# The seam between a recurrent-attention stage and a mixture-of-experts stage: one expert's rows loaded ahead of the last scatter, that scatter's rows added on TensorE

## The chip, the cores and the metric

The kernel runs on one core of a Trainium2 chip. The metric is the device time of one execution in microseconds (us), the median of several runs. All times inside the execution are counted from the start of the profiled span.

## What is computed

Three layers follow each other. The first is a recurrence over 768 steps for 4 batches of 8 heads, whose output becomes 3072 token rows of 320 numbers. The second sends each token to the expert with the largest logit, in order of arrival up to a capacity (768), and weights the expert's result with the softmax probability. The third is a dense two-layer network with an ELU.

```python
y[:, :, t] = einsum('bhd,bhde->bhe', rt, state)
Sa = einsum('bhde,bhe->bhd', state, at)
state = state * wt[:, :, None, :] - einsum('bhd,bhe->bhde', Sa, bt) + einsum('bhd,bhe->bhde', vt, kt)
...
expert_idx = argmax(x @ w_gate, axis=1)          # x: 3072 x 320, 8 experts
disp[e, counts[e]] = x[i]                        # rows of expert e in order of arrival
h = maximum(einsum('ecd,edf->ecf', disp, w1), 0) # 8 x (320 -> 1024 -> 320)
y = einsum('ecf,efd->ecd', h, w2)
out[i] = gate_w[i] * y[expert_idx[i], pos[i]]
...
h = x @ w_in                                     # 320 -> 2048 -> 320, all tokens
return where(h > 0, h, exp(minimum(h, 0)) - 1) @ w_out
```

## The kernel before

**First stage (`attention`).** The recurrence is cut into 24 units of work (two groups of heads, chunks of 64 steps), and each unit into steps with one-letter names: `q` and `y` are the products that give the output, `x` turns it into 128 token rows with their gate logits (a tile `XO` of 329 columns: 320 numbers, the token's number, 8 logits), `b` and `j` find each row's place (`SLOT`), `D` scatters `XO` with an indirect transfer on GpSimd's queue into `disp`, the array in HBM that holds each expert's rows. The order of all steps is written down by hand: a table `ORDER` for the early units and a function `slot(k)` that writes the later ones. Every engine and queue executes its own instructions in just that order. Between them stand steps named `V`: pieces of a conversion of 64-bit weights into 32-bit ones on VectorE, seven blocks here, two or three VectorE instructions a piece, with loads and stores on SyncE's queue. Twenty-one of these pieces stand in units 17 to 23; the last one stands behind the last scatter `D23`. Steps of `ahead` prepare the first half of the first expert's weights (`fetch` loads a half, `split` cuts it into a high and a low part, a cast on ScalarE and four subtractions on GpSimd for each of four pieces).

**The seam.** When the first stage ends, its buffers are given back, and the second stage's buffers lie on the same memory: the first use of such a buffer on an engine waits until all that used the old ones is done.

**Second stage (`ffn`).** Blocks of rows follow each other: 8 experts of 448 rows (4 x 112), then 6 blocks of 512 tokens for the dense network. `start` loads the first block's rows `X` from `disp`, holds TensorE busy with 26 products whose result nobody reads, turns the rows with 12 transposes into three PSUM tiles `pt`, and `prep` casts them to `XH`/`XS` on ScalarE and takes the remainder `XL` on VectorE. `run` then makes, for each of the 8 quarters f of a block, the first products (`s1`, 8 matmuls into `ph`), the second products of the quarter three before (`s2`, 8 matmuls into `po`), the ReLU of the quarter before (ScalarE writes H, VectorE writes L), a step of the next block's load, softmax (`soft`, the gate of each row) and transposes, and a piece of `split` of later weights. For block b the next block's load stands at f = 0, its softmax at f = 2, the four multiplications of its rows by the gate (L1094, ScalarE) at f = 3, its transposes at f = 4, 5 and 6. The first block alone isn't multiplied before but after its products, by a tile made in `late_gate`.

Of the kernel before, what the change touches and what calls it, by code (L numbers as in the profile page):

```python
# [33 lines left out]
ORDER = """
se1 sa0 se0 se0 v1 sc0 e0.0 sv se1 e0.1 sd p0 sw p0 e1.0 sw a0 p0 v0 p1 sa1 sx a0 p1 lw sz st1 e2.0 c0.0 a1
p2 p2 a1 c0.0 e1.1 sr1 Z7 c0.1 p1 e3.0 c0.1 k0.0 k0.1 c0.1 c1.0 e2.1 a2 a2 c1.0 p3 c1.1 k1.1 k1.0 c1.1 k1.0 e4.0 d1 k1.1
c1.1 e3.1 m0.0 l0 m0.1 k0.1 p2 p3 a3 l1 a3 p4 p4 p3 m1.1 c2.1 e5.0 k2.1 c2.0 c2.1 m1.0 r0 c2.0 k2.0 k0.0 a4 m2.1 a4 p5
st0 k2.0 k3.1 sc1 c3.0 c2.1 c3.1 ss1 k3.0 e4.1 m2.0 p4 r0 r1 c4.0 i0 e6.0 k3.0 n0 k3.1 m3.0 k4.1 p5 n1 o0 c3.1 p6
c3.0 e5.1 a5 a5 c3.1 m3.1 k2.1 r1 e7.0 l2 p5 k4.1 c4.1 k4.0 m4.1 e6.1 c4.0 c5.1 k5.1 l3 p6 k5.0 c5.0 c4.1 p7 c4.1 p6 a6
m5.0 a6 v2 v3 p7 c5.0 t1 m4.0 t0 c6.1 m6.1 c5.1 k4.0 f1 k6.1 c5.1 k6.0 k6.1 m5.1 sr0 a7 i1 c6.0 f1 f0 a7 o1 e7.1 e8.0 f1 f0  # L40
k5.0 p7 c6.1 f0 f1 f1 p8 c6.0 d0 e9.0 f0 k5.1 c7.1 f0 f1 f1 c6.1 c7.0 f0 f0 e8.1 c7.1 g1 c7.0 g0 p8 m7.0 a8 ss0 p8 m7.1
g0 k7.1 l5 l4 g1 k7.0 k7.1 g0 k8.0 g0 c7.1 l6 p9 e9.1 g1 a8 u0 m6.0 p9 k6.0 k8.1 u0 g1 l7 c8.0 k7.0 m8.0 c8.1 n2 t2 e10
w0 a9 p9 f2 n3 k8.1 a9 q0.0 w0 q0.1 q0.1 w0 i2 u1 u1 f2 q0.0 c8.0 f2 p10 k9.1 c9.1 f2 c8.1 c9.0 m8.1 k8.0 Z2 c8.1 f2 w0
Z4 p10 t3 f2 s0 k9.1 p10 c9.1 c9.0 w1 w1 k9.0 y0 f2 i2 k9.0 g2 s0 w1 e11 s0 c9.1 f3 k10.1 Z3 r2 a10 w1 a10 f3 k10.1 m9.0
f3 y0 m9.1 k10.0 p11 Z0 r2 c10.0 q1.0 q1.0 c10.1 x0 f3 p11 h2 q1.1 s1 f3 g2 a11 k10.0 m10.1 i2 f3 c10.0 g2 q1.1 c10.1 h2
e12 v4 p11 f3 s1 c10.1 x0 y1 y1 d2 g3 p12 a11 s1 k11.1 c11.0 x1 g3 r3 Z6 c11.0 g2 g3 p12 k11.1 h3 x1 m11.0 a12 Z5 p12 x0 r3
u2 a12 c11.1 c12.0 u2 g3 w2 d3 c11.1 w2 k11.0 w2 x1 k12.1 h3 q2.0 q2.1 Z1 b0 w2 c11.1 c12.1 u3 c12.1 m10.0 m11.1 s2 j0
o2 u3 w3 k11.0 q2.1 q3.1 c12.0 e13 z2 q2.0 s2 w3 y2 s2 l11 j0 l10 y2 t4 m12.0 m12.1 r4 v5 l9 g4 d4 w3 k12.1 r4 p13 D0
h4 x2 l8 g4 c12.1 k12.0 D1 h4 t5 q3.0 p13 w3 g4 g4 g4 s3 u4 x2 a13 l12 s3 z3 q3.0 u4 w4 w4 a13 q3.1 p13 i3 w4 g5 h5 y3
d5 x2 w4 y3 s3 s4 i3 k12.0 e14 t6 s4 s4 h5 v6  # L50
"""
FIRST = [f for f, n in GROUPS if f > 6]
AHEAD = (17, 19, 20, 21, 22, 23)

CV0, CVN = 17, 7


def slot(k):
    L = []
    a = lambda x: L.extend(x.split())  # L60
    live = k < NU

    nx, up = k + 1, k + (8 if k < 7 else 9)
    ups = up < NU
    pair = k - 3 if k % 2 else None
    work = {f - 6 + i: (g, i) for g, (f, n) in enumerate(GROUPS) for i in range(4) if f > 8}
    work[5] = (3, 3)
    w = work.get(k)
    if live: a(f"r{k} r{k}")
    if ups and k != 7: a(f"c{up}.0")  # L70
    if FU <= k < NU: a(f"g{k} g{k}")
    more = ups and up + 1 < NU
    if ups and k != 7: a(f"m{up}.0 c{up}.0")
    if more and k != 7: a(f"p{up+1}")
    a(f"x{k-2} x{k-2} x{k-2}")
    if k == NU: a(f"b{NU-2}.1")
    if FU <= k < NU: a(f"g{k} g{k}")
    if w and w[1]:
        a(f"i{w[0]}")
        if w[1] == 3: a(f"o{w[0]}")  # L80
    if k % 2 == 0: a(f"D{k-3}")
    second = f"c{up}.1 m{up}.1 c{up}.1 c{up}.1 p{up+1} l{up}"
    if ups: a(second if k != 7 else f"a{up} a{up} c{up}.0 m{up}.0 c{up}.0 p{up+1}")
    if k + 2 < NU: a(f"v{k+2}")
    V = (lambda: a("V")) if CV0 <= k < NU else (lambda: None)

    if nx in FIRST: a(f"t{nx}")
    a(f"q{k-1}.0 q{k-1}.0")
    V()
    if w and not w[1] and k != 6: a(f"i{w[0]}")  # L90
    if live: a(f"u{k} u{k}")
    if k == 7: a(second)
    if more: a(f"p{up+1}")
    a(f"q{k-1}.1 q{k-1}.1")
    V()
    if pair is not None: a(f"b{pair}")
    if ups:
        a(f"k{up}.0 k{up}.0 k{up}.1 k{up}.1")
    if FU <= nx < NU and nx not in FIRST: a(f"g{nx}")
    if live and k < 22: a(f"w{k} w{k} w{k} w{k}")  # L100
    if up + 2 < NU: a(f"E{up+2}")
    if more: a(f"a{up+1} a{up+1}")
    a(f"z{k-1}")
    if nx < NU: a(f"h{nx} h{nx}")
    if nx < NU: a(f"d{nx}")
    if k + 2 < NU and k + 2 not in FIRST: a(f"t{k+2}")
    if live and k < 22: a(f"s{k} s{k} s{k}")
    if k == NU: a(f"j{NU-2}.1 j{NU-2}.1 D{NU-2}")
    a(f"y{k-1} y{k-1}")
    if nx in FIRST: a(f"g{nx}")  # L110
    V()
    if pair is not None: a(f"j{pair} j{pair} D{pair}")
    if k == 6:
        up += 1
        a(f"c{up}.0 m{up}.0 c{up}.0 c{up}.1 m{up}.1 c{up}.1 c{up}.1 p{up+1} l{up} i{w[0]}")
        a(f"k{up}.0 k{up}.0 k{up}.1 k{up}.1 E{up+2} p{up+1} p{up+1}")
    return " ".join(L)

# [1373 lines left out]
```

## Time and profile before

| | |
|---|---|
| median of 3 runs | 1049.12 us (1045.7 to 1049.5) |
| the profiled execution's own time | 1045.15 us |
| its span in the trace | 1043.3 us |
| busy in the span: TensorE matmuls | 959.6 us, 92% |
| VectorE | 726.0 us, 70% |
| GpSimd | 616.3 us, 59% |
| ScalarE | 515.7 us, 49% |
| mean granted TensorE clock | 0.942 of full |

PE is TensorE's matmuls, PEld its weight loads, DVE is VectorE, ACT ScalarE, POOL GpSimd, SPq SyncE's queue. Busy time is a sum over the span; the seam lies between 425 and 465 us, and what happens there is read from the timeline, not from the sums.

### The profile page before, as it was taken

The numbers are of one execution on the slowest core, as the hardware profiler recorded it, in microseconds if no ns is written. First come the engines' busy times: TensorE is split into PE (matmuls) and PEld (weight loads), VectorE is DVE, ScalarE is ACT, GpSimd is POOL, SyncE is SP. The second block draws the span as 40 slices with busy tenths as digits, with TensorE's granted clock in tenths as the row PEclk, the third lists the DMA queues.
The fourth block names the chain that finished last, engine by engine and source line by source line (L and its number), as shares of the span: only waits on it lengthen the run. The fifth ranks groups of instructions, "written<-read, shape, count | busy, mean of one in ns | idle before, by whom it ended". The sixth has DMA issues, their size and how long they took to land.

```text
span 1043.3 us, 25335 instructions
## 1 busy us (share of the span) xinstructions
PE 959.6 (92%) x9995; PEld 868.6 (83%) x9995; DVE 726.0 (70%) x1287; ACT 515.7 (49%) x1011; POOL 616.3 (59%) x926
## 2 busy tenths in 40 slices
PE   4868978899899999989999999999999999999993
PEld 4858878798788889778888888888999889998893
DVE  8956757788674568547677777586767777677761
ACT  3646535566464334254445556465545555455551
POOL 4767929899898813377768777944333323333332
PEclk8867878899899889999999999999999999999997
DMA  6768776666665674386786766601001010100000
GB/s 163 170 171 201 167 135 124 146 138 137 131 122 117 138 192 116 118 227 192 224 225 169 225 192 206 226 24 26 26 1 52 1 26 26 26 26 1 26 2 28
DMA packets 180935, 121.67 MB, mean 117 GB/s; under 512 B 105744, under 2 KB 166824, under 8 KB 179176
## 3 DMA queue, kind: packets, MB, share of 16 engines
...
HBM read 86.87 MB, written 33.05 MB: 115 GB/s over the span
## 4 chain that ended last, share of the span: by engine, by line
PE 40%; DVE 7%; DMA 3%; ACT 3%; issue 2%; POOL 1%; SPq 0%; POOLq 0%; ACTq 0%; DVEq 0%
PE ph L970 21%; PE po L998 5%; PE po L997 5%; PE po L996 5%; DMA w<-E 2%; DVE L L1101 2%; DVE E L859 1%; ACT X L1094 1%; ACT ring L775 1%; DVE M L865 1%; DMA ring<-in_w_dram 1%; DVE N L864 1%; POOL L L1115 1%; ACT H L1100 1%; PE po L1037 1%
## 5 line engine op out<-in xcount | busy, mean ns | idle before, releaser
L780 POOL TENSOR_TENSOR ring<-ring,ring 128x64 fp32r<-128x64 f32 (+2 forms) x320 | 203.9, 674 | 75.3 <-ACT ring L775 75.3
L1115 POOL TENSOR_TENSOR L<-E,H 128x512 fp32r<-128x512 f32 x66 | 90.7, 1374 | 169.7 <-ACT H L1114 155.9
L970 PE MATMUL ph<-XH,ring 128*128 128x512 f32 (+1 forms) x640 | 170.5, 388 | 0.6 <-ACT XH L954 0.3
L1108 ACT ACTIVATE E<-N 128x512 f32<-128x512 f32 x96 | 60.8, 633 | 151.1 <-DVE N L1107 78.2
L353 POOL TENSOR_TENSOR X<-X,ring 128x60 f32<-128x60 f32 (+19 forms) x170 | 125.5, 738 | 13.3
L970 PEld LDWEIGHTS ph<-XH,ring 128*128 128x128 f32 x640 | 115.7, 189 | 14.7 <-ACT XH L954 0.6
L998 PE MATMUL po<-ring,L 128*128 128x320 f32 x384 | 119.4, 311 | 1.5 <-POOL L L1115 1.5
L996 PE MATMUL po<-ring,H 128*128 128x320 f32 x384 | 118.5, 309 | 0.2 <-ACT H L1114 0.2
L997 PE MATMUL po<-ring,H 128*128 128x320 f32 x384 | 118.5, 309 | 0.0
L970 PE MATMUL ph<-XL,ring 128*128 128x512 f32 (+1 forms) x320 | 96.7, 383 | 0.0
L970 PE MATMUL ph<-XS,ring 128*128 128x512 f32 (+1 forms) x320 | 96.5, 382 | 0.0
L351 POOL TENSOR_TENSOR ring<-X,ring 128x60 f32<-128x60 f32 (+19 forms) x108 | 69.8, 646 | 39.4 <-DMA ring<-dab 18.3
L1112 DVE SCALAR_TENSOR_TENSOR M<-E,M 128x512 f32<-128x512 f32 x96 | 79.4, 827 | 14.8 <-ACT M L1109 14.7
L1107 DVE TENSOR_SCALAR N<-ph 128x512 f32<-128x512 f32 x96 | 65.7, 684 | 27.9 <-PE ph L970 27.6
L996 PEld LDWEIGHTS po<-ring,H 128*128 128x128 f32 x384 | 72.1, 188 | 4.5 <-ACT H L1114 0.5
L997 PEld LDWEIGHTS po<-ring,H 128*128 128x128 f32 x384 | 71.9, 187 | 4.3
L998 PEld LDWEIGHTS po<-ring,L 128*128 128x128 f32 x384 | 72.1, 188 | 2.0 <-POOL L L1115 2.0
L1113 DVE SCALAR_TENSOR_TENSOR E<-ph,M 128x512 f32<-128x512 f32 x96 | 66.4, 691 | 8.1 <-DVE M L1112 0.5
L970 PEld LDWEIGHTS ph<-XL,ring 128*128 128x128 f32 x320 | 60.8, 190 | 10.9
L1101 DVE SCALAR_TENSOR_TENSOR L<-ph,H 128x448 fp32r<-128x448 f32 x64 | 39.4, 617 | 43.5 <-ACT H L1100 43.4
L970 PEld LDWEIGHTS ph<-XS,ring 128*128 128x128 f32 x320 | 60.2, 188 | 10.5
L775 ACT CAST ring<-ring 128x704 fp32r<-128x704 f32 x80 | 61.4, 778 | 12.4 <-DMA w<-GE 5.7
...
## 6 DMA issues: line engine op xcount, KB each, us to landing
...
```

Source lines behind the costliest of these rows:

```text
L351: nc.gpsimd.tensor_tensor(tv, X[:, 0:n, s:s + 1].to_broadcast([128, n, m]), N[:, s:s + 1, s + 1:e].to_broadcast([128, n, m]), op=ALU.mult)
L353: nc.gpsimd.tensor_tensor(X[:, 0:n, s + 1:e], X[:, 0:n, s + 1:e], tv, op=ALU.subtract)
L775: s.nc.scalar.copy(B[:, 0:704], r)
L780: s.nc.gpsimd.tensor_tensor(B[:, to], r[:, q], B[:, q].bitcast(F32), op=ALU.subtract)
L970: nc.tensor.matmul(p, l, r[:, 0:s.T], start=i == 0, stop=i == len(seq) - 1)
L996: nc.tensor.matmul(o, H[:, c], hb, start=f == 0, stop=False)
L997: nc.tensor.matmul(o, H[:, c], lb, start=False, stop=False)
L998: nc.tensor.matmul(o, L[:, c], hb, start=False, stop=f == s.W.nf - 1)
L1107: nc.vector.tensor_scalar(N, p, 0.0, None, op0=ALU.min)
L1112: nc.vector.scalar_tensor_tensor(out=M, in0=E, scalar=1.0, in1=M, op0=ALU.add, op1=ALU.mult)
L1113: nc.vector.scalar_tensor_tensor(out=E, in0=p, scalar=0.0, in1=M, op0=ALU.max, op1=ALU.add)
L1115: eng.tensor_tensor(L, E, H.bitcast(F32), op=ALU.subtract)
```

## The change

Five edits, all around the seam.

1. The table now holds the whole order, and is otherwise the old one, except: the pieces `V` of the last two units are closer together, so that the piece that stood behind `D23` and the one behind `y22` now stand between `q22` and `b20`; and the first half of `j22` stands before `y`'s first products of unit 23.
2. `D23` is taken out of the first stage. Unit 23's row tile is no longer one of the four `XO` buffers but a part of `DR`, which moves to the constants, so that it outlives the first stage.
3. `last_rows`: the first expert's rows are loaded (in four transfers of 112 rows instead of one of 448) without unit 23's rows, whose places hold zeros. A matrix of zeros and ones says which of unit 23's tokens belongs in which of the 448 places.
4. In `start`, 10 unread products instead of 26; then, into each of the three `pt` tiles, two products of the 0/1 matrix with the high and low part of unit 23's rows, and on top of them the loaded rows by 12 products with the identity instead of 12 transposes. `last_scatter` (the old `D23`) stands on GpSimd's queue behind the four pieces of `split(1)`.
5. `late_gate` loads the first expert's logits by themselves, after the last scatter, and its softmax and products are later (f = 5 of the first block to f = 1 of the second); of `split(2)` no piece stands at f = 0 and two stand at f = 2 and 3.

```diff
-        XO = wk.tile([128, RW], F32, tag="XO", name="XO", bufs=4)
+        XO = DR[:, 0:RW] if u == NU - 1 else wk.tile([128, RW], F32, tag="XO", name="XO", bufs=4)
...
     do(f"x{NU-1}", f"b{NU-1}.1")
     warm(6)
-    do( f"j{NU-1}.1", f"D{NU-1}", "V")
+    do(f"j{NU-1}.1")
...
+            if add:
+                oh, parts = add
+                w = [slice(128 * k, 128 * k + (128, 128, s.W2)[k]) for k in range(3)]
+                for k, c in enumerate(w):
+                    for j, x in enumerate(parts):
+                        nc.tensor.matmul(P[k][0:c.stop - c.start, 0:s.T], x[:, c], oh[:, 0:s.T], start=j == 0, stop=False)
+                for i in range(4):
+                    for k, c in enumerate(w):
+                        nc.tensor.matmul(P[k][0:c.stop - c.start, s.P * i:s.P * i + s.P], s.X[0:s.P, i, c], ident[0:s.P, 0:s.P], start=False, stop=i == 3)
...
-            nc.sync.dma_start(out=s.X[0:112], in_=src)
+            for i in range(4) if now else (slice(0, 4),):
+                nc.sync.dma_start(out=s.X[0:112, i], in_=src[:, i])
...
+        add = None if dyn else last_rows(bl[0])
         go(split(1), 5)
-        bl[0].start(0 if dyn else 26)
+        if not dyn:
+            last_scatter()
+        bl[0].start(0 if dyn else 10, add)
...
-            go(gen[0], 1 if i < 14 else 2)
+            go(gen[0], (0, 1, 2, 2)[f] if i == 0 and not dyn else 1 if i < 14 else 2)
...
+    def last_rows(B):
+        xo = cst["dr"][:, 0:RW]
+        it = ap.tile([128, 512], F32, tag="N", name="N")[:, 0:SL]
+        oh, xh, xl = (ap.tile([128, 512], F32R, tag="H", name="H", bufs=6) for _ in range(3))
+        w = slice(0, D + 1)
+        nc.gpsimd.iota(it, pattern=[[1, SL]], base=SL, channel_multiplier=0, allow_small_or_imprecise_dtypes=True)
+        nc.scalar.copy(xh[:, w], xo[:, w])
+        nc.gpsimd.tensor_tensor(xl[:, w], xo[:, w], xh[:, w].bitcast(F32), op=ALU.subtract)
+        for _ in B.load(True):
+            pass
+        f = ap.tile([128, 1], F32, name="sf", bufs=1)
+        nc.vector.tensor_copy(f, cst["slot"][:, 23:24])
+        nc.vector.tensor_scalar(oh[:, 0:SL], it, f, None, op0=ALU.is_equal)
+        return oh, (xh, xl)
...
     def late_gate(B):
-        g = yield from soft(B, "late")
+        yield
+        lg = ap.tile([128, 4, 8], F32, name="lgx", bufs=1)[0:112]
+        with nc.allow_non_contiguous_dma("the logits of a row"):
+            nc.sync.dma_start(out=lg, in_=dv[0, 1][:, :, D + 1:RW])
+        yield
+        yield
+        yield
+        g = yield from soft(B, "late", lg)
```

How it moves instructions, at the three places that matter below. First VectorE in unit 23's turn, from the mask of `q22`'s second half (`Qs`) to unit 22's output `XT`; before:

```order
L530 TENSOR_TENSOR Qs_6185<-q_6208,mask_63 128x512
L858 TENSOR_SCALAR GE1_94<-AM5_132 128x320
L859 SCALAR_TENSOR_TENSOR GE3_96<-AM5_132,GE1_94 128x320
L580 TENSOR_REDUCE mx_6217<-LG_68 128x2
...
L556 TENSOR_TENSOR XT_139<-y_6227,GE10_103 104x512
L864 TENSOR_SCALAR GE1_94<-GE3_96 128x320
L865 SCALAR_TENSOR_TENSOR GE2_95<-AM5_132,GE1_94 128x320
```

And with the change (L812 to L824 are the conversion's lines there, L486 is `Qs`, L536 begins `b20`, L512 is `XT`):

```order
L812 TENSOR_SCALAR GE1_95<-AM5_132 128x320
L813 SCALAR_TENSOR_TENSOR GE3_97<-AM5_132,GE1_95 128x320
L486 TENSOR_TENSOR Qs_6185<-q_6211,mask_63 128x512
L818 TENSOR_SCALAR GE1_95<-GE3_97 128x320
L819 SCALAR_TENSOR_TENSOR GE2_96<-AM5_132,GE1_95 128x320
L821 TENSOR_TENSOR GE2_96<-GE2_96,GE3_97 128x320
L823 TENSOR_SCALAR GE1_95<-AM5_132 128x320
L824 SCALAR_TENSOR_TENSOR GE3_97<-GE1_95,GE2_96 128x320
L536 TENSOR_REDUCE mx_6223<-LG_68 128x2
...
L512 TENSOR_TENSOR XT_139<-y_6233,GE10_104 104x512
```

Five conversion instructions that stood behind `XT` (two) and behind the last scatter (three) now stand ahead of `b20` and `XT`. Second GpSimd's queue at the seam with the change (`one`, `begin`, `turn` are small constants of the second stage, `ring4` is the half of the weights that `split(1)` cuts, L1243 the last scatter):

```order
L1418 MEMSET one_6400 128x8
L1421 IOTA begin_6402 128x1 x4
...
L1425 MEMSET turn_6409 128x1
L1232 IOTA N_6411 128x448
L1234 TENSOR_TENSOR H_6414<-DR_73,H_6413 128x321
L734 TENSOR_TENSOR ring4_6426<-ring3_6270,ring4_6426 128x64
...
L1243 DMA disp_74<-DR_73,SLOT_70 28672x329
L734 TENSOR_TENSOR ring6_6529<-ring0_6491,ring6_6529 128x64
```

Before, the scatter (L610) stood directly ahead of `one`; now it stands behind two new instructions and the 16 of `split(1)`. Third SyncE's queue with the waits of each transfer, the second block's load `X` before and, in the second fence, with the change (`DMASW` are the semaphores of GpSimd's scatters):

```order
L1087 DMA X_6512<-disp_73 112x4x329 [waits DMAHW3_49,DMAHW5_49,DVE_49,PE_49]
L801 DMA ring3_6514<-in_w1_dram 128x4x128 [waits Activation_49,Pool_49]
```

```order
L1053 DMA X_6508<-disp_74 112x4x329 [waits DMAHW6_49,DMAHW0_49,DMAHW7_49,DMASW5_49,PE_49]
L755 DMA ring3_6510<-in_w1_dram 128x4x128 [waits Activation_49,Pool_49]
```

The scatter's semaphore is now waited for by the second block's load instead of the first block's, and `fetch(3)` (`ring3`) stands behind that wait.

## Rows read from the trace of the kernel before

**Rows 1.** Busy time by stretch of 100 us (stretch, length, engines with counts, clock, DMA)
```profile
500.00:600.00 100.00, 97.12 (x490) 86.27 (x489) 74.42 (x136) 49.41 (x91) 73.85 (x115) 1.00 0.74 214
```
**Rows 2.** Timeline of TensorE, 434 to 464 us (start, length, instruction, idle before)
```profile
434.50 1.12 PE L562 MATMUL x<-IW,XT 128*128 128x88 f32 x8 [0.79 <-DVE XT L556]
...
447.31 1.71 PE L935 MATMUL pt<-ident,X 112*128 112x112 f32 x12 [3.13 <-DMA X<-disp]
...
449.31 1.92 PE L970 MATMUL ph<-XH,ring 128*128 128x448 f32 x4 [0.29 <-ACT XH L954]
...
452.08 0.98 PE L970 MATMUL ph<-XH,ring 128*128 128x448 f32 x4
...
462.89 0.55 PE L935 MATMUL pt<-ident,X 112*128 112x112 f32 x4
463.71 1.08 PE L970 MATMUL ph<-XH,ring 128*128 128x448 f32 x4 [0.27 <-DVE L L1101]
```
**Rows 3.** Stretches of 2 us: TensorE busy, granted clock, DMA share, GB/s
```profile
448.00:450.00 2.00, 1.71 (x9) 0.53 1.16 227
450.00:452.00 2.00, 2.00 (x8) 0.62 0.65 204
```
**Rows 4.** Timeline of VectorE, 425 to 440 us
```profile
425.30 0.69 DVE L530 TENSOR_TENSOR Qs<-q,mask 128x512 f32<-128x512 f32 x1 [0.31 <-PE q L525]
...
426.67 0.16 DVE L580 TENSOR_REDUCE mx<-LG 128x2 f32<-128x16 f32 x1
...
427.78 0.68 DVE L556 TENSOR_TENSOR XT<-y,GE 104x512 f32<-104x512 f32 x1
428.38 0.32 DVE L864 TENSOR_SCALAR GE<-GE 128x320 int32<-128x320 int32 x1
428.73 0.49 DVE L865 SCALAR_TENSOR_TENSOR GE<-AM,GE 128x320 f32<-128x320 uint32 x1
429.14 0.17 DVE L601 TENSOR_TENSOR rt<-rt,ebase 128x16 f32<-128x16 f32 x1
...
438.31 0.48 DVE L867 TENSOR_TENSOR GE<-GE,GE 128x320 f32<-128x320 f32 x1
...
439.06 0.49 DVE L870 SCALAR_TENSOR_TENSOR GE<-GE,GE 128x320 f32<-128x320 int32 x1
```
**Rows 5.** Timeline of GpSimd, SyncE's queue and ScalarE, 439 to 452 us
```profile
439.02 0.96 POOL L610 DMA_INDIRECT disp<-XO,SLOT  x1 [3.92 <-issue]
...
441.75 2.82 ACT L775 CAST ring<-ring 128x704 fp32r<-128x704 f32 x4 [5.66 <-DMA w<-GE]
442.47 0.34 SPq L1087 DMA_DIRECT2D X<-disp  x1
442.78 0.10 POOL L1418 MEMSET one<- 128x8 f32 x1 [2.69 <-issue]
...
443.30 8.35 POOL L780 TENSOR_TENSOR ring<-ring,ring 128x64 fp32r<-128x64 f32 x16
...
451.77 0.34 SPq L1087 DMA_DIRECT2D X<-disp  x1
```
**Rows 6.** Timeline of VectorE and ScalarE, second block's softmax and gate
```profile
456.36 0.17 DVE L1074 TENSOR_REDUCE g<-X 112x4 f32<-112x32 f32 x1
...
457.32 0.77 ACT L775 CAST ring<-ring 128x704 fp32r<-128x704 f32 x1
...
459.96 1.93 ACT L1094 ACTIVATE X<-X,g 112x320 f32<-112x320 f32 x4 [1.43 <-DVE rn L1350]
```
**Rows 7.** Groups by shape, 441 to 460 us (count, busy us, mean ns, idle before)
```profile
L780 POOL TENSOR_TENSOR ring<-ring,ring 128x213 fp32r<-128x213 f32 x14 | 8.7, 644 | 0.0
...
L1263 PE MATMUL pgate<-ident,g 112*128 112x112 f32 x8 | 1.0, 273 | 0.0
```
**Rows 8.** Groups by shape, GpSimd, whole span
```profile
L1115 POOL TENSOR_TENSOR L<-E,H 128x512 fp32r<-128x512 f32 x66 | 90.7, 1374 | 169.7 <-ACT H L1114 155.9 <-PE po L997 9.5 <-PE ph L970 4.3
```
**Rows 9.** The 24 scatters of the first stage, from issue to landing
```profile
DMA to landing us min/median/max: 2.7/4.8/7.6
```

More of the change, by code (lines that the diff above doesn't have):

```diff
@@ L39 @@
[L39 to L43, printed above, removed]
@@ L49 @@
-h4 x2 l8 g4 c12.1 k12.0 D1 h4 t5 q3.0 p13 w3 g4 g4 g4 s3 u4 x2 a13 l12 s3 z3 q3.0 u4 w4 w4 a13 q3.1 p13 i3 w4 g5 h5 y3
-d5 x2 w4 y3 s3 s4 i3 k12.0 e14 t6 s4 s4 h5 v6
-"""
[L52 to L117, printed above, removed]
@@ L145, in attention @@
     zr = sh[0][:, 2578:2798]
-    DR = one.tile([128, 520], F32, name="DR")
+    DR = cst["dr"]
     NPC = LOOK + 4
@@ L637, in attention @@
                  n=m_load, t=tt_load, f=t32, g=t64, r=rhs, u=u_solve, w=vu_tr, s=s_update, h=s_tr, q=q_mm, z=y_state, y=y_mm, x=x_out,
-                 b=route, j=route_mm, D=scatter, Z=zero_d, V=lambda: cv.pieces(spare, CVN))
+                 b=route, j=route_mm, D=scatter, Z=zero_d, X=zero_x, V=lambda: cv.pieces(spare, CVN))
     def spare(i, words):
@@ L652, in go @@
     def go(key):
+        if key == "A":
+            next(early, None)
+            return
         if key not in open_:
@@ L668, in attention @@
         go(key)
-    for k in range(KR, NU + 1):
-        for key in slot(k).split():
-            go(key)
-        for _ in range(AHEAD.count(k)):
-            next(early, None)
-        if k == 8:
-            zero_x()
     for _ in early:
@@ L683, in attention @@
     ctx.close()
+    return sent
 def consts(p):
@@ L699, in consts @@
     c["cap"] = p.tile([128, 2], I32, name="CAP")
+    c["dr"] = p.tile([128, 520], F32, name="DR")
     return c
@@ L883, in ahead, with ffn @@
     W.fetch(1)
-def ffn(tc, nc, cst, disp, xt, w1, w2, w32, out, ring, W0, cv):
+def ffn(tc, nc, cst, disp, xt, w1, w2, w32, out, ring, W0, cv, sent_x):
     ident = cst["ident"]
@@ L915, in load, with start @@
             yield from s.fload(s, now)
-        def start(s, busy=0):
-            for _ in s.load(True):
-                pass
+        def start(s, busy=0, add=None):
+            if not add:
+                for _ in s.load(True):
+                    pass
             if busy:
@@ L925, in start @@
             P = [ps.tile([128, 512], F32, tag="ph", name="pt") for _ in range(3)]
-            for i in range(4):
-                for k in range(3):
-                    s.turn(P[k], i, k)
+            if add:
[7 more added lines that the diff above has]
+                        nc.tensor.matmul(P[k][0:c.stop - c.start, s.P * i:s.P * i + s.P], s.X[0:s.P, i, c], ident[0:s.P, 0:s.P], start=False, stop=i == 3)
+            else:
+                for i in range(4):
+                    for k in range(3):
+                        s.turn(P[k], i, k)
             for _ in s.prep(P):
@@ L1067, in prep, with soft @@
                 yield
-    def soft(s, tag="s"):
+    def soft(s, tag="s", lg=None):
         t = lambda nm, sh: ap.tile(sh, F32, tag=tag + nm, name=nm, bufs=1)[0:112]
         g, x = t("g", [128, 4]), t("x", [128, 4, 8])
-        lg = s.X[0:112, :, D + 1:RW]
+        lg = s.X[0:112, :, D + 1:RW] if lg is None else lg
         nc.vector.tensor_reduce(g, lg, axis=AX.X, op=ALU.max)
@@ L1240, in extra @@
                 return
-            if b == 0 and f > 1:
+            if b == 0 and f > 1 or b == 1 and f < 2:
                 next(first, None)
@@ L1255, in experts, with last_scatter @@
         run(bl, extra)
-    def late_gate(B):
-        g = yield from soft(B, "late")
+    def last_rows(B):
[7 more added lines that the diff above has]
+        for _ in B.load(True):
+            pass
+        f = ap.tile([128, 1], F32, name="sf", bufs=1)
+        nc.vector.tensor_copy(f, cst["slot"][:, 23:24])
+        nc.vector.tensor_scalar(oh[:, 0:SL], it, f, None, op0=ALU.is_equal)
+        return oh, (xh, xl)
+    def last_scatter():
+        x = nc.gpsimd.indirect_dma_start(
+            out=disp, out_offset=bass.IndirectOffsetOnAxis(ap=cst["slot"][:, 23:24], axis=0),
+            in_=cst["dr"][:, 0:RW], in_offset=None).ins
+        for y in sent_x:
+            tc.declare_no_dep(x, y, reason="scatters write different rows")
+    def late_gate(B):
+        yield
[6 more added lines that the diff above has]
+        g = yield from soft(B, "late", lg)
+        yield
         yield
@@ L1463, in network @@
         W0, cv = expert(nc, ring, w1, w2, 0), Convert(nc, w_in, w_out, w32)
-        attention(tc, nc, e_in, v_tok, d_in, wg, disp, xt, cst, ring, ahead(W0), W0, cv, cap)
-        ffn(tc, nc, cst, disp, xt, w1, w2, w32, out, ring, W0, cv)
+        sent = attention(tc, nc, e_in, v_tok, d_in, wg, disp, xt, cst, ring, ahead(W0), W0, cv, cap)
+        ffn(tc, nc, cst, disp, xt, w1, w2, w32, out, ring, W0, cv, sent)
 def layout(r, k, v, w, a, b, moe_w_gate, moe_w1, moe_w2, moe_capacity, moe2_w_in, moe2_w_out):
```

48 lines of the change are left out of this document (38 added, 10 removed).

## The prediction

> **What bounds the kernel now.** I read the stretches first. From the second stage on TensorE is busy for 97.12 of 100 us at full clock [rows 1], so there the time is TensorE's work: a delay that TensorE takes at the seam is carried to the end, and one that another engine takes counts only where TensorE comes to wait for it. Then the timeline of the seam, engine by engine. Unit 23's token rows leave TensorE at 434.50 + 1.12 = 435.62, and the second stage's first product starts at 449.31 [rows 2]: 13.7 us, the chain of which is VectorE's routing (until the last conversion piece can start, 438.31 [rows 4]), the scatter at 439.02, the load of the first rows at 442.47 when the scatter has landed [rows 5], the transposes at 447.31 after 3.13 us of waiting for that load, and the casts. This is what the change works on. Afterwards TensorE runs to the second block's transposes at 462.89 and waits 0.27 us ahead of the product at 463.71 [rows 2]; those transposes need the second block's rows, loaded at 451.77 [rows 5], their softmax from 456.36, and the four multiplications 459.96 to 461.89 [rows 6]. They are ready 1.0 us before TensorE comes. I call this second chain the block-two chain; it is the nearest wait that could take the place of the first.
>
> **Part 1, the conversion pieces.** On VectorE `Qs` at 425.30 had waited 0.31 us, and from there to `XT` at 427.78 VectorE has no idle time; TensorE waits for `XT`, there as in the next unit (0.79 us [rows 2]). The change puts five instructions ahead of `XT`: two that took 429.14 − 428.38 = 0.76 us, and three that took 439.55 − 438.31 = 1.24 us [rows 4]. Less the 0.31 us that was idle anyway, `XT` comes 0.76 + 1.24 − 0.31 = 1.7 us later. From `XT` of unit 22 the chain goes on without a place to make it up (x, logits, routing, mask, y, `XT` of unit 23, x, routing), because it is in each step a TensorE product waiting for VectorE or the reverse. Routing ends at 438.3 + 1.7 = 440.0 in the place of 438.3. Bounds: 0.8 us, if the waits of that chain absorb part, to 2.0. What the piece behind the scatter gave up: ScalarE's casts of `split(1)` waited for its store until 441.75 [rows 5]; now they start earlier, which is worth nothing by itself, since these weights are first used at f = 4.
>
> **Part 2, the first rows.** Their load no longer waits for the last scatter, but the buffer's memory still belongs to the first stage until routing ends, so it is issued at about 440.2 instead of 442.47, a gain of 2.3 us. Four issues of 0.34 us [rows 5] are out by 441.6. The whole block took 442.47 to 447.31, 4.84 us; the scatter, a quarter of the bytes, was waited for 442.47 − 439.98 = 2.5 us after its issue. The last quarter lands at 444.1 to 446.4; I take 445.0. TensorE meanwhile: ten unread products and the six 0/1 products, all of 448 to 512 columns at 0.25 us (0.98 for four [rows 2]), from 440.0 to about 444.0 with the matrix of zeros and ones ready by 442. The 12 products with the identity are not transposes: a product of this kind is two records of the trace, and four of them took 1.0 us [rows 7], so 12 take 3.1 us where the transposes took 1.71. They end at 447.0 (bounds 446.0 to 447.5); the transposes ended at 449.02. The gain is 2.0 us, and the first product's eight matmuls get faster too. Ahead of them TensorE had idled 3.13 us, and the granted clock was 0.53 and 0.62 of 2.4 GHz, near its lower level, from 448 to 452 [rows 3], where 2.77 us passed to the second product at 452.08. With work until 444 I expect full clock and 2.1 us. The second product starts at 449.4, a **gain of 2.7 us** (1.5 to 3.2).
>
> **Part 3, the last scatter and the block-two chain.** The scatter moves behind everything that GpSimd does at the seam. From 440.0: 0.7 us until GpSimd reacts (438.31 to 439.02), 0.52 us of small constants (442.78 to 443.30), the two new instructions, then 8.35 us of `split(1)` [rows 5]. The trace has no row for the iota of 448 columns or a subtraction of 321; a subtraction of 213 columns took 0.64 us [rows 7], one of 512 columns 1.37 [rows 8], so the two cost between 0.8 and 2.7 us. I take 1.4. The scatter is issued at 440.0 + 0.7 + 0.5 + 1.4 + 8.35 = 451.0, and has landed 3.45 us later, as it did from 439.02 to 442.47: 454.4. The second block's load now waits for it, and behind it `fetch(3)` on SyncE's queue. It was issued at 451.77; now 454.5. It needs at most 456.36 − 451.77 = 4.59 us: 459.1 (457.0, if 2.5 us do). From the first softmax instruction to the end of the multiplications it was 461.89 − 456.36 = 5.53 us [rows 6]; ScalarE now has one cast more in between (0.77 us there), VectorE less: 5.9. The rows are ready at 465.0, and the product behind the transposes starts at **465.3 instead of 463.71, 1.6 us later** (bounds: 1.0 us earlier to 3 us later).
>
> TensorE comes to these transposes early: it took 462.89 − 452.08 = 10.8 us from the second product, of which 0.8 us for the first block's gate products goes elsewhere, so it is there at 449.4 + 10.0 = 459.4 and waits some 5 us. That is a longer gap than the 3.13 us after which the clock was low. What the low clock cost there is 4 − 2 x 0.53 − 2 x 0.62 = 1.7 us of work [rows 3]; here TensorE has full work behind the gap, so it counts. Bounds 0 (the gap is shorter or the clock stays) and 1.7; I take 1.6.
>
> The Trainium skill ("TensorE: Matmul & The Clock Gate", Why this matters for your kernels) says that idle gaps between bursts of matmuls bring the clock back to half. The trace agrees with 0.53 after 3.13 us. By that rule the change trades one gap for another, and speaks against it.
>
> The Trainium skill ("DMA: Bandwidth & Descriptors", Anatomy of one DMA) gives a transfer on GpSimd's path about 2.0 us plus its bytes over 436 GB/s. An estimate by that page: 2.4 us for the scatter's 168 KB, where 2.5 were read; 3.4 us for the block's 590 KB, where the timeline bounds it by 4.59. By it the chain would come 1.2 us sooner, and the sum with it.
>
> **Part 4, the rest.** `late_gate`'s work is moved by 5 quarters and hidden under TensorE's products there; the logits' load stands in SyncE's queue ahead of `fetch(4)`, which has more than 5 us to spare. `fetch(1)` is issued some 3 us later, behind the last conversion's store; its data are first wanted by casts at 440. Hidden as long as it lands within 8 us of its issue; if not, `split(1)`, and so the scatter, comes later by as much.
>
> **The sum.** The gain of 2.7 us at the second product is lost in the wait for the second block's rows. Counted at the product behind it: +1.6 us of the chain, +1.6 us of clock, together +3.2 us. The profiled execution's own time is 1045.15 us, so 1048.35. That execution is at the fast end: the median of the runs shown is 4.0 us above it, their highest 4.4.
>
> **Rivals.** *The gain stays.* If the block-two chain is 5 us shorter than I read it (the scatter issued earlier, the load done in 2.5 us, the softmax in less), TensorE doesn't wait at the second block and the 2.7 us are kept: 1042.4. For it: several terms are upper bounds. Against: the 8.35 us of `split(1)` alone ahead of the scatter. Between the two, with part of the wait and a full clock, lies 1044 to 1046.
>
> *Slower.* The scatter lands late. Its 24 fellows took 2.7 to 7.6 us [rows 9], 3.45 is at the low end. If `fetch(2)`'s 1.4 MB, issued from 441.7, are still under way at 451, it takes up to 7.6, 4.15 us more, all of which the block-two chain passes on: 1048.35 + 4.15 = 1052.5. It decides for slower from a landing of 5.5 us on (3.45 + 5.2 − 3.2). Against: before, `fetch(2)` and the load shared the queues until about 452, and now they start 2 us sooner.
>
> *The change doesn't do what it says*: the load waits for something else of the first stage as long as it waited for the scatter. Then the gain at the seam is nought, the block-two chain is as above, and the time the forecast's, since the chain doesn't hang on that load.
>
> **Chances.** My forecast, a few us slower at most: 0.50. The gain kept, or part of it: 0.32. The late scatter: 0.13. The third: 0.05. A measurement of this kernel can tell about 0.5%, 5.2 us, from no change. No case saves 5.2 us by its sum; with a part I have mis-sized I leave 0.07 for faster. For slower 0.14: the late scatter, and little from the forecast's tail. That leaves 0.79 for the same. The range reaches from the kept gain, 1042.4, to the late scatter, 1052.5, widened by 0.5 us above for runs that lie above the profiled one: 1042.4 to 1053.0.
>
> **What would show it.** In the profile after: five conversion instructions ahead of unit 22's `XT`, and `XT` 1.7 us later against `Qs`; the first load about 2 us after that routing's end rather than after a scatter; 24 records of identity products taking 3 us; the second product some 2.7 us earlier; the scatter behind 16 subtractions and the second block's load right after its landing; an idle time of 4 to 5 us on TensorE ahead of that block's transposes, released by the gate's multiplications, with a low clock behind. The prediction is wrong if that idle time isn't there, or is twice as long.

## The result and the profile after

| | before | with the change |
|---|---|---|
| median, 22 runs each | 1047.39 us (1037.91 to 1055.68) | 1053.17 us (1045.66 to 1061.9) |
| ratio, 95% interval | | 1.0053 [1.0036, 1.007] |
| the profiled execution's own time | 1045.15 us | 1051.98 us |
| its span | 1043.3 us | 1050.2 us |
| mean granted TensorE clock | 0.942 | 0.938 |

The change makes the kernel slower by 0.53%. The forecast was 1048.35 us, that is 3.2 us more than the profiled execution; the range ended at 1053.0, and the median lies 0.17 us above it. The forecast had been added to that one profiled execution; the median of the 22 executions of the kernel before lies 2.2 us above it.

**A common zero.** The part of the first stage ahead of the seam ends at another time in each execution, whatever the kernel: the instant named next lies between 421.19 us, in a run of the changed kernel, and 429.71 us, in one of e4's. So the traces are compared from one fixed instruction: the mask of the first half of `q22` on VectorE (`Qs`). Here is VectorE's timeline of the kernel before, with the instruction that ends routing (L607), and then that of the changed kernel (L563 ends routing; of the five conversion instructions ahead of `XT` the first is shown, L818; L1039 is the first instruction that reads the second block's rows).

```profile
423.13 0.69 DVE L530 TENSOR_TENSOR Qs<-q,mask 128x512 f32<-128x512 f32 x1 [0.85 <-PE q L525]
...
438.24 0.15 DVE L607 TENSOR_TENSOR ACC<-ACC,roh 128x8 bf16<-128x8 bf16 x1
```

```profile
424.88 0.69 DVE L486 TENSOR_TENSOR Qs<-q,mask 128x512 f32<-128x512 f32 x1 [0.86 <-PE q L481]
...
428.15 0.32 DVE L818 TENSOR_SCALAR GE<-GE 128x320 int32<-128x320 int32 x1
...
431.30 0.68 DVE L512 TENSOR_TENSOR XT<-y,GE 104x512 f32<-104x512 f32 x1
...
444.36 0.16 DVE L563 TENSOR_TENSOR ACC<-ACC,roh 128x8 bf16<-128x8 bf16 x1
462.75 0.19 DVE L1039 TENSOR_REDUCE g<-X 112x4 f32<-112x32 f32 x1 [6.01 <-DMA X<-disp]
```

Unit 22's `XT` came 427.78 − 423.13 = 4.65 us after the zero [rows 4] and comes 6.42 after it now: 1.77 us later, where 1.7 were foreseen. But routing ends 444.36 − 424.88 = 19.48 us after the zero, and ended at 438.24 − 423.13 = 15.11: 4.4 us later, not 1.7. TensorE's timeline shows what happens in between, with a stretch of 2 us; first of the kernel before:

```profile
427.72 0.18 PE L597 MATMUL rt<-roh,tri 128*128 128x16 bf16 x1 [0.51 <-DVE roh L587]
...
428.52 1.12 PE L562 MATMUL x<-IW,XT 128*128 128x88 f32 x8 [0.43 <-DVE XT L556]
429.48 1.98 PE L525 MATMUL q<-RVU 128*128 128x128 f32 x16
```

```profile
428.00:430.00 2.00, 1.57 (x14) 1.48 (x14) 1.76 (x8) 0.32 (x1) 0.00 (x1) 1.00 0.84 217
```

Then of the changed kernel:

```profile
431.25 0.18 PE L553 MATMUL rt<-roh,tri 128*128 128x16 bf16 x1 [2.28 <-DVE roh L543]
...
432.04 2.01 PE L518 MATMUL x<-IW,XT 128*128 128x88 f32 x8 [0.43 <-DVE XT L512]
433.84 3.69 PE L481 MATMUL q<-RVU 128*128 128x128 f32 x16
...
440.63 1.12 PE L518 MATMUL x<-IW,XT 128*128 128x88 f32 x8 [0.80 <-DVE XT L512]
...
446.92 1.46 PE L886 MATMUL pt<-H 128*128 128x448 f32 x6 [0.28 <-issue]
448.22 2.70 PE L889 MATMUL pt<-ident,X 112*128 112x112 f32 x24
451.13 1.30 PE L935 MATMUL ph<-XH,ring 128*128 128x448 f32 x4 [0.21 <-ACT XH L919]
...
453.49 0.98 PE L935 MATMUL ph<-XH,ring 128*128 128x448 f32 x4
...
467.17 1.81 PE L900 MATMUL pt<-ident,X 112*128 112x112 f32 x4 [3.69 <-ACT X L1060]
468.65 1.84 PE L935 MATMUL ph<-XH,ring 128*128 128x448 f32 x4
...
473.65 0.55 PE L900 MATMUL pt<-ident,X 112*128 112x112 f32 x4
```

TensorE now waits 2.28 and 0.43 us for VectorE in unit 22's turn, where it waited 0.51 and 0.43 us, and the products behind that wait are slow: the eight of `x22` take 2.01 us and those of `q23` 3.69, where they took 1.12 and 1.98. The stretches of 2 us (their eighth value is the granted clock, 1.00 in the one of the kernel before) show the low clock there, and show it a second time behind the wait of 3.69 us for the second block's rows:

```profile
432.00:434.00 2.00, 1.96 (x9) 1.96 (x10) 0.56 (x5) 0.00 (x0) 1.12 (x2) 0.50 0.84 207
434.00:436.00 2.00, 2.00 (x11) 2.00 (x11) 1.25 (x9) 0.43 (x1) 1.08 (x2) 0.50 0.98 238
436.00:438.00 2.00, 2.00 (x16) 1.92 (x16) 1.04 (x3) 0.00 (x0) 0.00 (x0) 0.50 1.00 330
...
470.00:472.00 2.00, 2.00 (x7) 1.78 (x6) 1.93 (x6) 1.11 (x2) 2.00 (x5) 0.50 0.03 11
```

0.50 is the lower of the two levels, 1.2 GHz. If the first low stretch is what lies between the two delays, it costs 4.4 − 1.8 = 2.6 us (e5 below tests this), and it stands in no term of the prediction. The second is the 1.6 us foreseen in Part 3: from the product at 468.65 to the second transposes 5.0 us pass, and before it was 43.97 − 40.58 = 3.39 (43.97 from the table below, 40.58 is 463.71 − 423.13, [rows 2]); e6 tests that.

GpSimd's and SyncE's rows answer to [rows 5]:

```profile
444.71 1.76 SPq L1053 DMA_DIRECT2D X<-disp  x4
...
445.21 0.51 POOL L1232 IOTA N<- 128x448 f32 x1
445.69 0.88 POOL L1234 TENSOR_TENSOR H<-DR,H 128x321 fp32r<-128x321 f32 x1
446.52 8.56 POOL L734 TENSOR_TENSOR ring<-ring,ring 128x64 fp32r<-128x64 f32 x16
455.23 1.00 POOL L1243 DMA_INDIRECT disp<-DR,SLOT  x1
...
458.14 0.35 SPq L1053 DMA_DIRECT2D X<-disp  x1
```

From here on the positions of all kernels, counted from the common zero in their profiled executions (us): the end of routing, the first block's second product, the second block's first and second transposes (from the second ones on TensorE has its rows and its steady work goes on), and the ratio of times to the kernel before.

| kernel | routing ends | 2nd product | 1st transposes | 2nd transposes | ratio [95%] |
|---|---|---|---|---|---|
| before | 15.11 | 28.95 | 39.76 | 43.97 | 1 |
| change | 19.48 | 28.61 | 42.29 | 48.77 | 1.0053 [1.0036, 1.007] |
| change again (e8) | 18.23 | 27.37 | 41.34 | 48.66 | 1.0037 [1.0008, 1.0065] |
| e1 pieces only | 18.49 | 33.19 | 44.70 | 48.35 | 1.0021 [0.9992, 1.0049] |
| e2 pieces back | 15.01 | 24.15 | 37.92 | 45.12 | 1.0011 [0.9981, 1.0042] |
| e3 scatter early | 19.31 | 28.43 | 39.39 | 44.17 | 0.999 [0.9965, 1.0016] |
| e4 both, first | 15.00 | 24.31 | 34.72 | 39.49 | 0.9996 [0.9963, 1.0029] |
| e4 again | 15.01 | 24.14 | 35.28 | 41.61 | 0.9952 [0.9924, 0.9979] |
| e4 third | 15.00 | 24.12 | 34.75 | 39.53 | 0.9972 [0.9946, 0.9998] |
| e5 first wait filled | 16.80 | 25.94 | 41.31 | 47.30 | 1.0008 [0.9984, 1.0033] |
| e6 second filled | 18.24 | 27.37 | 41.20 | 45.97 | 1.0032 [1.0009, 1.0054] |
| e7 both filled | 16.79 | 25.93 | 41.09 | 47.42 | 1.0033 [1.0006, 1.0061] |
| e9 first partly filled | 18.25 | 27.38 | 41.53 | 48.82 | one run |
| e10 e4, second filled | 15.01 | 24.18 | 34.92 | 39.57 | 0.9985 [0.9953, 1.0016] |

At the second transposes the change stands 4.8 and 4.7 us behind the kernel before; its two ratios are worth 5.6 us (3.8 to 7.3 by the interval) and 3.9 (0.8 to 6.8). Within these intervals the seam accounts for the result.

### The profile page after: what moved, and what is told of

Same layout as the page of the kernel before. It is cut to its first block, busy times and chain, and to the rows that moved or that the text cites. A ratio compares the mean times of both kernels' runs of the same rounds, so it can differ in the third digit from the quotient of the medians.

```text
span 1050.2 us, 25348 instructions
## 1 busy us (share of the span) xinstructions
PE 960.9 (91%) x9997; PEld 869.4 (83%) x9997; DVE 727.7 (69%) x1289; ACT 516.1 (49%) x1012; POOL 617.8 (59%) x927
## 4 chain that ended last, share of the span: by engine, by line
PE 61%; DVE 13%; DMA 9%; issue 6%; POOL 5%; ACT 4%; SPq 1%; POOLq 0%; ACTq 0%; DVEq 0%
PE ph L935 20%; PE po L962 5%; PE po L963 5%; PE po L961 5%; PE q L481 4%; DMA ring<-in_e_in_dram 3%; PE sc L233 2%; PE ut L425 2%; PE x L518 2%; PE st L450 2%; DMA TA<-dx 2%; PE y L495 2%; DVE L L1067 1%; DVE ring L199 1%; DMA w<-E 1%
## 5 line engine op out<-in xcount | busy, mean ns | idle before, releaser
L309 POOL TENSOR_TENSOR X<-X,ring 128x60 f32<-128x60 f32 (+19 forms) x170 | 110.8, 652 | 13.3
L307 POOL TENSOR_TENSOR ring<-X,ring 128x60 f32<-128x60 f32 (+19 forms) x108 | 73.7, 683 | 42.6 <-DMA ring<-dab 18.8
L1080 ACT CAST H<-E 128x512 fp32r<-128x512 f32 x96 | 59.1, 616 | 14.9 <-DVE E L1079 11.7
```

The costliest lines, as they stand in the source:

```text
L307: nc.gpsimd.tensor_tensor(tv, X[:, 0:n, s:s + 1].to_broadcast([128, n, m]), N[:, s:s + 1, s + 1:e].to_broadcast([128, n, m]), op=ALU.mult)
L309: nc.gpsimd.tensor_tensor(X[:, 0:n, s + 1:e], X[:, 0:n, s + 1:e], tv, op=ALU.subtract)
```

## The experiments

My theory after the two traces, called A: two waits of TensorE, each with a stretch of low clock behind it, eat what the earlier load wins; the pieces of the conversion make the first, the late scatter the second. The rival for the first is that VectorE's own extra work delays routing and the clock only follows; for the second, that the products behind the wait are slow because they wait for their operands.

### e1: the pieces alone

The kernel before, with the conversion pieces where the change puts them.

```
-    V = (lambda: a("V")) if CV0 <= k < NU else (lambda: None)
+    V = (lambda: a("V V" if k == NU - 1 else "V")) if CV0 <= k < NU else (lambda: None)
...
-    do( f"j{NU-1}.1", f"D{NU-1}", "V")
+    do( f"j{NU-1}.1", f"D{NU-1}")
```

> The kernel before with the conversion pieces of the change's table alone (two more of them ahead of unit 22's XT, none behind the last scatter). Theory A (two waits of TensorE, each with a stretch of low clock behind it, ate the gain of the early load): XT comes 1.8 us later against the mask of q22, TensorE waits some 2.3 us there, the granted clock falls to 0.5 for about 5 us, and routing ends 4.4 us later: about +4.4 us, ratio 1.004. Rival B (the low clock at this place was a chance of the one trace, the pieces cost what VectorE takes): +1.7 us, ratio 1.0015. Rival C (the pieces cost nothing; the loss lies elsewhere in the first stage, in the buffer that was moved): 0, ratio 1.000.

Measured: 1052.62 us beside 1048.99, ratio 1.0021 [0.9992, 1.0049]. TensorE's timeline and a stretch show the same wait and the same low clock, without any other part of the change:

```profile
431.52 0.18 PE L597 MATMUL rt<-roh,tri 128*128 128x16 bf16 x1 [2.27 <-DVE roh L587]
...
432.32 1.76 PE L562 MATMUL x<-IW,XT 128*128 128x88 f32 x8 [0.43 <-DVE XT L556]
```

```profile
434.00:436.00 2.00, 2.00 (x11) 2.00 (x11) 1.22 (x9) 0.43 (x1) 1.23 (x4) 0.50 0.86 224
```

Routing ends 3.4 us later than before and at the second transposes TensorE is about 4.4 us late. The time's interval can't tell that from nothing; the trace can.

### e2: the change with the pieces back

The pieces of the last two units at their old places, the last one behind `y23`.

```
-... q22.0 q22.0 V V u23 u23 q22.1 q22.1 V V b20 z22 y22 y22 V V
-j20 j20 D20 A ... D22 z23 y23 y23
+... q22.0 q22.0 V u23 u23 q22.1 q22.1 V b20 z22 y22 y22 V
+j20 j20 D20 A ... D22 z23 y23 y23 V
```

> The changed kernel with the conversion pieces at their old places, the last one behind unit 23's XT, where VectorE had 1.7 us of idle time. Theory A: routing ends 4.4 us earlier and everything behind it too, 4.4 us less than the change, about +1.4 us against before, ratio 1.001. Rival B: 1.7 us less than the change, +4.1 us, ratio 1.004. Rival C: as the change, 1.0055.

Measured: 1049.86 us beside 1048.99, ratio 1.0011 [0.9981, 1.0042]. TensorE's timeline:

```profile
429.78 0.18 PE L553 MATMUL rt<-roh,tri 128*128 128x16 bf16 x1 [0.51 <-DVE roh L543]
...
449.34 0.96 PE L935 MATMUL ph<-XH,ring 128*128 128x448 f32 x4
...
463.11 1.81 PE L900 MATMUL pt<-ident,X 112*128 112x112 f32 x4 [3.80 <-ACT X L1060]
```

Without the moved pieces TensorE waits 0.51 us in unit 22, the clock there is 1.00, and routing ends as before (15.01). The second product comes 28.95 − 24.15 = 4.8 us earlier than before: this is the whole worth of the early load, with the faster first product. All of it and 1.2 us more are gone at the second transposes, behind 3.80 us of waiting for the second block's rows.

### e3: the change with the scatter early

```
-        go(split(1), 5)
+        cut = split(1)
+        go(cut, 5 if dyn else 1)
         if not dyn:
             last_scatter()
+            go(cut, 4)
```

> The changed kernel with the last scatter behind the first of the four pieces of the weight split on GpSimd instead of behind all four. Theory A: the scatter is issued 6.4 us earlier, the second block's load with it, and TensorE's wait of 3.7 us ahead of that block's transposes goes, with the low clock behind it (1.6 us): 5.3 us less than the change, about +0.5 us against before, ratio 1.0005. Rival D (that wait is the load's and the softmax's own length, not the scatter's place, or the scatter then waits for the first load on GpSimd and delays the split as much): at most 2 us less than the change, ratio 1.0035 or more.

Measured: 1049.06 us beside 1048.99, ratio 0.999 [0.9965, 1.0016]. GpSimd, SyncE's queue and TensorE in its timeline, and a stretch:

```profile
448.59 0.99 POOL L1245 DMA_INDIRECT disp<-DR,SLOT  x1
...
455.13 0.35 SPq L1053 DMA_DIRECT2D X<-disp  x1
...
464.06 1.68 PE L900 MATMUL pt<-ident,X 112*128 112x112 f32 x4 [0.99 <-ACT X L1060]
```

```profile
466.00:468.00 2.00, 2.00 (x11) 1.87 (x10) 1.49 (x3) 2.00 (x5) 1.89 (x4) 1.00 0.22 42
```

The scatter is issued 6.4 us earlier (counted from the zero, 23.92 against 30.35), and TensorE's wait falls from 3.69 to 0.99 us; behind it the clock stays at 1.00. The second transposes come at 44.17 in the place of 48.77. So the late scatter was the second wait's cause. Of the 6.4 us only 2.8 reach the second block's load (30.46 against 33.26): the scatter, which landed after 2.9 us in the changed kernel, takes 6.5 us here, beside the transfers of `fetch(2)`.

### e4: both, three times

e2's and e3's edits together.

> The changed kernel with both: conversion pieces at their old places (the last behind unit 23's XT) and the last scatter behind the first piece of the split. Theory A: both waits are gone and the early load's gain of 2.7 us and more is kept, about -4 us against before, ratio 0.996. Rivals B and D: little better than the better of the two alone, ratio 1.002. Rival C: 1.000 or more.

> Once more the kernel with the pieces at their old places and the last scatter after the first piece of split(1), to narrow its interval. Theory A: no wait over 1 us and no low clock at the seam, 4.4 us won at the second block's transposes, and if the later blocks lose nothing the time is 1044 to 1046 beside 1048 of the kernel before. Rival (about 2 us of it are given back behind the seam, where later blocks' rows come late): 1046 to 1048.

> The kernel with the pieces back and the scatter early a third time, since its two intervals, [0.9963, 1.0029] and [0.9924, 0.9979], hardly overlap. By the traces it stands 4.4 to 2.4 us ahead of the kernel before at the second transposes of block two and loses 0 to 2 us behind: ratio 0.996 to 0.999. Rival: 0.9952 was the truth and 0.995 comes again, or nothing is won and it is 1.000.

Measured: 1047.23, 1048.41 and 1044.28 us beside 1048.99, 1051.92 and 1048.37; ratios 0.9996 [0.9963, 1.0029], 0.9952 [0.9924, 0.9979] and 0.9972 [0.9946, 0.9998]. The second transposes come 4.5, 2.4 and 4.4 us earlier than in the kernel before. The middle one is the one whose wait grew over 1 us, and there the clock fell once more, as TensorE's timeline and a stretch of that run show. Behind them stand those of the third run, with GpSimd's row of the scatter:

```profile
460.51 1.68 PE L900 MATMUL pt<-ident,X 112*128 112x112 f32 x4 [1.17 <-ACT X L1060]
```

```profile
464.00:466.00 2.00, 2.00 (x7) 1.79 (x6) 1.62 (x5) 0.46 (x2) 2.00 (x5) 0.50 0.05 8
```

```profile
446.01 1.00 POOL L1245 DMA_INDIRECT disp<-DR,SLOT  x1 [0.58 <-DMA X<-disp]
...
460.71 1.68 PE L900 MATMUL pt<-ident,X 112*128 112x112 f32 x4 [0.55 <-ACT X L1060]
```

```profile
464.00:466.00 2.00, 2.00 (x14) 1.77 (x13) 1.86 (x5) 0.67 (x2) 2.00 (x5) 1.00 0.09 22
```

The scatter can hardly be sooner: it waits 0.58 us for the first load, which must have read the rows that it overwrites. This version's ratio lies below the changed kernel's each time, and below that of the kernel before in two of three comparisons by more than the interval.

### e5, e9: the first wait filled, wholly and in part

Nine, or four, products whose result nobody reads, behind unit 22's second products of `y`.

```
-... b20 z22 y22 y22 V V
+... b20 z22 y22 H y22 V V
...
+                 H=lambda: warm(9),
```

> The changed kernel with nine unread products of 512 columns put on TensorE behind unit 22's second products, where it waited 2.28 us. Theory A (the wait brought the clock down, and the low clock cost the 2.6 us that the forecast lacked): unit 22's XT still comes 6.4 us after Qs, but the granted clock stays at 1.00 from XT to the end of q23, x22 and q23 take about 1.1 and 2.0 us instead of 2.01 and 3.69, routing ends 16.9 us after Qs instead of 19.5, the product behind the second block's transposes stands at 41.2 instead of 43.8, and the time is 2.6 us less than the changed kernel's 1053.2: about 1050.6. Rival (the delay is VectorE's own work or its port, and the clock only follows): routing ends at 19.5 again, and the time is 1053.

> The changed kernel with four unread products instead of nine behind unit 22's second products, so that about 1.3 of the 2.28 us of waiting are left. Theory A: if a wait of that size is enough, the clock falls to 0.50 behind it as in the changed kernel and routing ends 19 us or more after Qs; if not, it stays at 1.00 and routing ends 16.9 us after Qs, as with nine. The rival (VectorE's own work) expects 19.5 us whatever the clock.

Measured: e5 1053.8 us beside 1051.92, ratio 1.0008 [0.9984, 1.0033]; e9, one run, 1054.11. TensorE and a stretch of e5, then of e9:

```profile
431.51 2.34 PE L590 MATMUL warm<-ring 128*128 128x512 f32 x9
...
434.66 1.12 PE L518 MATMUL x<-IW,XT 128*128 128x88 f32 x8 [0.43 <-DVE XT L512]
435.62 1.98 PE L481 MATMUL q<-RVU 128*128 128x128 f32 x16
```

```profile
436.00:438.00 2.00, 2.00 (x21) 1.80 (x21) 1.51 (x9) 0.25 (x1) 1.59 (x4) 1.00 1.02 256
```

```profile
432.94 0.18 PE L553 MATMUL rt<-roh,tri 128*128 128x16 bf16 x1 [1.15 <-DVE roh L543]
...
433.73 1.75 PE L518 MATMUL x<-IW,XT 128*128 128x88 f32 x8 [0.43 <-DVE XT L512]
```

```profile
434.00:436.00 2.00, 2.00 (x12) 2.00 (x12) 0.34 (x4) 0.42 (x1) 1.37 (x3) 0.51 0.97 243
```

This settles the first rival. In e5 unit 22's `XT` is as late as in the changed kernel (6.43 us), VectorE has the same work, and only the clock differs: routing ends at 16.80, 1.69 us later than before, which is the bare delay of the pieces. With 1.15 and 0.43 us of waiting left (e9, one execution) the clock falls all the same, and routing ends at 18.25, as in e8 with the whole wait (18.23).

The forecast for the second transposes failed, though: of 2.7 us won at the second product, only 1.5 were left there. SyncE's queue and VectorE show why:

```profile
457.92 0.35 SPq L1053 DMA_DIRECT2D X<-disp  x1
...
464.38 0.19 DVE L1039 TENSOR_REDUCE g<-X 112x4 f32<-112x32 f32 x1 [7.48 <-DMA X<-disp]
```

The second block's load took 6.46 us here, and 6.09 in e7, where the changed kernel's took 462.75 − 458.14 = 4.61. What made it slow is not shown, but these two traces have something that the other twelve haven't: a small transfer of the instruction queue (0.02 MB) falls into the load's time, and SyncE's four issues of `fetch(3)` behind the load take 3.94 us in e5 and 3.38 in e7, where they take 2.2 to 2.3 elsewhere. e5's ratio is 0.45 and 0.29% below the change's two, that is 4.7 and 3.0 us where its trace leaves 1.5 and the forecast was 2.6; its time alone would not have decided.

### e6, e7, e10: the second wait filled

Fourteen unread products (four in e10) on TensorE ahead of the second block's first transposes; e7 has e5's nine too, and e10 is e4 with them.

```
+                if b == 0 and f == 4 and isinstance(B, Turned):
+                    p = ps.tile([128, 512], F32, tag="po3", name="busy", bufs=1)
+                    for _ in range(14):
+                        nc.tensor.matmul(p, W0.B[0][:, 0:128], W0.B[0][:, 0:512], start=True, stop=True)
                 if b + 1 < n and next(first, 1) and f >= nf - 6:
```

> The changed kernel with fourteen unread products on TensorE ahead of the second block's first transposes, where it waited 3.69 us. Theory A: the product behind the transposes stands at 43.8 us after Qs as in the changed kernel, but the clock behind it is 1.00 instead of 0.50, from it to the second transposes pass 3.4 instead of 5.0 us, and the time is 1.6 us less: about 1051.6. Rival (those 1.6 us are waits of the products on VectorE's or ScalarE's halves, not the clock): 5.0 us again and 1053; and if the unread products outlast the wait, the product is later by as much.

> Both fills together. Theory A: the two low clocks are independent prices, 2.6 and 1.6 us: product behind the second block's transposes at 41.2 us after Qs, second transposes at 44.6 (changed kernel 48.8, kernel before 44.0), time about 1049.0, that is within 1 us of the kernel before. Rival: one of the two prices isn't the clock's, and the time stays at 1051 or above.

> The kernel with the pieces back and the scatter early, with four unread products of 512 columns ahead of the second block's first transposes, where TensorE waited 0.43 and 1.17 us. Theory A: the clock behind stays at 1.00 and up to 1.6 us are won where it fell, up to 0.5 us lost where the rows came first; ratio to the same kernel without them between 0.998 and 1.000. Rival: the clock falls behind a wait of that size or not by chance, and the fill costs 0.4 us.

Measured: e6 1054.45 us and e7 1054.83 beside 1051.92, ratios 1.0032 [1.0009, 1.0054] and 1.0033 [1.0006, 1.0061]; e10 1046.49 beside 1048.37, 0.9985 [0.9953, 1.0016]. e6's TensorE and a stretch:

```profile
467.04 1.68 PE L900 MATMUL pt<-ident,X 112*128 112x112 f32 x4 [0.65 <-ACT X L1060]
...
471.81 0.55 PE L900 MATMUL pt<-ident,X 112*128 112x112 f32 x4
```

```profile
470.00:472.00 2.00, 2.00 (x12) 1.75 (x11) 1.93 (x6) 0.99 (x2) 2.00 (x5) 1.00 0.02 7
```

With the wait filled but for 0.65 us, the clock is 1.00, and from the first to the second transposes 4.77 us pass; in the changed kernel it was 6.48, in e8 7.32. The second rival falls: the products are slow by the clock. The times can't show it: e6's ratio is 0.21 and 0.05% below the change's two, where 1.6 us less, 0.15%, were expected, and the intervals overlap. The low clock behind this wait is worth 1.2 us (5.99 in e5, less 4.77) to 2.6 (e8). In e7 the load was slow, 1.97 us of waiting were left behind the fill, and 6.33 us passed: the fill missed, and e7 stayed 2.9 us above the kernel before (medians), where less than 1 us was expected. e10 gives e4's positions and no more: the wait that it fills had not brought the clock down in two of e4's three traces. It shows no gain over e4.

### e8: the change once more

> The change once more, unedited, beside the kernel before and e4 on one chip. If the seam alone sets the difference (5 us at the second block's second transposes), the ratio is 1.005 again and e4's lies 0.5 to 0.9% below it; if the first measurement was high by chance, it comes nearer to 1.002.

Measured: 1053.52 us beside 1048.37, ratio 1.0037 [1.0008, 1.0065]; e4, in the same comparison, is 0.65% below it. Slower again, and again 4.7 us behind at the second transposes.

## Why the prediction was wrong

**Part 1, the step that failed.** "From `XT` of unit 22 the chain goes on without a place to make it up" carried 1.7 us unchanged from `XT` to the end of routing, with 2.0 as the upper bound. It was 4.4. The delay itself was right to a tenth: 1.77 us at `XT`, 1.69 us at routing's end when the clock is held up (e5). What the step left out is TensorE's side of the same delay. VectorE's five instructions made TensorE wait 2.28 us instead of 0.51, the granted clock fell to 0.50, and `x22` and `q23`, which stand in the chain, ran at that level: 2.6 us more (1.4 us in e8). I had weighed the low clock at the block-two gap and not at the other wait that the change makes longer, the one in Part 1 itself.

**Part 2** had its sum right, if Part 1 is kept apart. The second product was to come 2.7 us earlier, with 1.7 us of Part 1 in it; e2, without Part 1, shows 4.8 (4.4 foreseen). In the changed kernel the gain shrinks to 0.34 us, since 1.8 us and 2.6 us of Part 1 come off it (4.8 − 4.4). The 24 identity records took 2.70 us where 3.1 were said, and the first product came at full clock, as forecast (2.36 us to the second one, 2.1 said).

**Part 3** held. Iota and subtraction cost 1.39 us (1.4 said), `split(1)` 8.56 (8.35), the scatter landed 2.9 us after its issue (3.45), the load took 4.61 us (at most 4.59). From routing's end to the product behind the second block's first transposes, 24.3 us passed where 465.3 − 440.0 = 25.3 were said. Without Part 1's 2.6 us the product would have come 0.6 us later than before, inside the bounds; with them it was 43.77 − 40.58 = +3.2. The wait there was 3.69 us (4 to 5 said), and the clock behind it cost the 1.6 us that I took. The prediction drew an estimate of 3.4 us for the load from the Trainium skill ("DMA: Bandwidth & Descriptors", Anatomy of one DMA). The trace disagrees, with 4.61 us here and 6.46 in e5; the Trainium skill's figure there is for transfers that GpSimd issues, and SyncE issues this one. For the scatter, which GpSimd issues, the estimate was 2.4 us and the trace has 2.9.

**The sum** was +3.2 us and the traces show +4.8; the 1.6 us between are Part 1's 2.6 less about 1.0 of a shorter chain. The range's lower side was spent on cases in which the gain stays, and none of its cases had a second low clock.

**The base** was low as well. The sum was added to 1045.15 us, one execution, of which the prediction itself says that it lies at the fast end, and the range was widened above by only 0.5 us for that. The median of 22 is 1047.39. So of the 4.8 us between 1048.35 and 1053.17, 2.2 are the base, 1.6 the sum's, and 1.0 is not found at the seam (5.8 us between the medians, 4.8 in the traces). That this total equals the +4.8 of the traces is chance. With the median as base the range would have reached 1055.2 and held the result even without a term for Part 1's low clock. The median lies near the late scatter's 1052.5, but not by that mechanism.

**The rivals.** "The gain stays" is not what happened, but e4 is that case made true: with the first wait as before and the second down to 0.43 to 1.17 us, the kernel is ahead of before by 2.4 to 4.5 us at the seam. "The scatter lands late" is refuted for the change (2.9 us). That the load would still wait for something else is refuted by its issue 0.35 us after routing's end.

**What stays open.** Behind the second transposes the traces differ by up to 5.4 us with no edit there: 574.7 to 578.4 us to the end of the span between the three runs of e4 alone. Part of it are three waits of TensorE in the last dense block, which are the same in all traces (0.24 or 0.25, 0.79 or 0.80 and 0.66 to 0.69 us, one after another) and after which the clock falls in some and not in others. A stretch of the changed kernel shows it low:

```profile
1030.00:1032.00 2.00, 2.00 (x10) 2.00 (x9) 0.00 (x0) 0.43 (x1) 0.69 (x1) 0.50 0.20 82
```

In the kernel before and in e4's third run the clock behind the same waits stays at 1.00, and in e4's first it falls. What the rest is, is not shown. Together with the first stage, whose end moves by 8.5 us between executions, this scatter leaves a ratio of 12 executions uncertain by some 0.3%, and it may be why the first ratio of e4 does not show what its trace does.
